# A decode step of attention and MLP on one core: first load ahead of the engines' parts, the last wait behind them, and the result turned by TensorE

## The chip, the core and the metric

The kernel runs on one NeuronCore of one Trainium2 chip. The core has five engines with instruction streams of their own: TensorE (PE; its weight loads are shown as PEld), VectorE (DVE), ScalarE (ACT), GpSimd (POOL) and SyncE (SP), which here only issues transfers. Transfers run on 16 DMA engines. The engines meet through semaphores. The metric is the device time of one execution in microseconds (us), as the median of several.

## What is computed

One token x (512 values) goes through two branches that are mixed by a gate. Branch A is attention with 32 heads over a cache of 4096 keys and values per head (head size 128); branch B is an MLP with a squared ReLU. All arrays are bfloat16.

```python
g = sigmoid((x * gate_w).sum(-1, keepdims=True))
q = (x @ wq).reshape(B, Sq, Hq, Dh)              # 512 -> 32 heads of 128
scores = einsum("bhqd,bhkd->bhqk", q, k) * (Dh ** -0.5)
p = softmax(scores, axis=-1)
a = einsum("bhqk,bhkd->bhqd", p, v).reshape(B, Sq, Hq * Dh) @ wo
h = relu(x @ w1 + b1)
b = (h * h) @ w2 + b2
return g * a + (1 - g) * b                       # 512 values, 1 KB
```

Each value of the caches is used once. What has to be read is 32 heads of 1 MB of keys and 1 MB of values, 4 MB each of `wq` and `wo`, and some 2.8 MB of MLP weights: 78.3 MB in all.

## The kernel before

Every engine's program is written out by hand, with a part for each engine inside one block (`nc.Block()`, line 248). Ahead of the block stands the opening of the program: a few constants set by GpSimd, and a meeting of all engines (line 733 in the profile). Behind the block all engines drain and meet once more; the profile shows this under line 103.

SyncE's part (lines 251 to 294) issues the large loads in the order in which they are needed: four loads of `wq` (line 254, 128 rows of 8 KB each, 1 MB), then seven heads of keys, then values and keys in turn (lines 260 and 265), with the MLP's and `wo`'s loads set in between (lines 277 to 290). Loads into a buffer in use wait for the engines that read it. At the very end SyncE waits for `s_f4`, issues the store of the result (line 292), and waits for `s_out`, which the store raises when it has landed (line 294).

ScalarE issues four small loads at the start (lines 340 to 343): x, `gate_w`, `b1`, and `b2` as 4 rows of 256 bytes. TensorE, VectorE and ScalarE work head by head: half of the scores of a head are made by VectorE (line 629), the other half by TensorE, which transposes key blocks into PSUM buffers `KP` (line 427, copied out by ScalarE at line 361) and multiplies. The sums over the values follow seven heads behind (line 463).

All terms of the result are summed in one PSUM tile `acc`, 128 x 4 (four columns of 128 values): the output projection (lines 507, 525, 531, 537) and the MLP's second layer (line 546). The last loads to land are those of `w2` (lines 287 to 290), so that line 546 comes last on TensorE.

The result is brought out by VectorE. It adds `b2` (already times 1 - g) into column 0 of each of four 32-wide groups of the tile `fin`, 128 x 4 x 32, whose rest was set to zero at line 597. Then it transposes `fin` in blocks of 32 x 32 (line 719) into `finT`, after which the wanted values stand in rows 0, 32, 64 and 96, each row with four runs of 32 values. The store gathers these 16 runs of 64 bytes.

Line 513 is a step used below for comparison: it transposes `onorm`, 128 x 8, on TensorE into 8 rows of 128 in PSUM, and VectorE copies them to SBUF at line 712.

Of the kernel before, what the change touches and what calls it, by code (L numbers as in the profile page):

```python
# [5 lines left out]
def bass_gated_mix__gqa_block_cached__dense_activation_squared_relu__decode_kernel(  # L6
# [22 lines left out]
    bf16 = mybir.dt.bfloat16  # L29
    ALU = mybir.AluOpType  # L30
# [47 lines left out]
    def turns():  # L78
        at, out = 0, []
        for _, e, k, _, _ in RUNS:  # L80
            d = (e - at) % 16
            out.append((False, d) if d != 1 else (True, e))
            at = (e + k) % 16
        return out
# [11 lines left out]
    wq_v = A_wq.rearrange("(p t) n -> p t n", t=4)  # L96
# [5 lines left out]
    ctx = ExitStack()  # L102
    with ctx:
        def sb(name, shape, dt):
            return ctx.enter_context(nc.sbuf_tensor(name, shape, dt))

        def pb(name, shape, dt):
            return ctx.enter_context(nc.psum_tensor(name, shape, dt))

        def sem(name):  # L110
            return ctx.enter_context(nc.semaphore(name))
# [4 lines left out]
        wq_sb = W[:, :].rearrange("p (t n) -> p t n", t=4)  # L116
# [17 lines left out]
        oB = sb("oB", [NH - NA, 128], bf16)  # L134
        o2A = sb("o2A", [128, 32], bf16)
        o2B = sb("o2B", [128, TB], bf16)
        finT = sb("finT", [128, 128], bf16)
        zeros = sb("zeros", [128, 128], bf16)
        xb = sb("xb", [128, 4, 128], bf16)
        dm = xb[:, :, :].rearrange("p t (n a c) -> p (t n) a c", a=2, c=16)  # L140
        ident = sb("ident", [128, 128], bf16)
# [17 lines left out]
        hr = sb("hr", [128, FG + 1], fp32)  # L159
        hs = sb("hs", [128, FG + 1], bf16)  # L160
        b2g = sb("b2g", [128, 4], fp32)
        fin = sb("fin", [128, 4, 32], bf16)

        KP = [pb(f"KP{i}", [128, HB * 128], bf16) for i in range(3)]
        pS = pb("pS", [128, 512], fp32)
# [16 lines left out]
        acc = pX[:, 256:260]  # L182
# [13 lines left out]
        s_wq = [sem(f"s_wq{t}") for t in range(4)]  # L196
# [9 lines left out]
        s_oT = sem("s_oT")  # L206
        s_oc = sem("s_oc")
        s_o2 = sem("s_o2")
        s_f4 = sem("s_f4")
        s_k = [sem(f"s_k{i}") for i in range(NK)]  # L210
        s_v = [sem(f"s_v{i}") for i in range(NV)]
# [33 lines left out]
        s_fin = sem("s_fin")  # L245
        s_out = sem("s_out")

        block = ctx.enter_context(nc.Block())


        @block.sync
        def _(eng):
            for t in range(4):
                eng.dma_start(wq_sb[:, t, :], wq_v[:, t, :]).then_inc(s_wq[t], 16)  # L254

            def load_k(h):
                if h >= NK:
                    eng.wait_ge(s_sd, h - NK + 1)
                    eng.wait_ge(s_t, 2 * (h - NK + 1))
                eng.dma_start(Kt[:, h % NK, :], k_h[h, :, :]).then_inc(s_k[h % NK], 16)  # L260

            def load_v(h):
                if h >= NV:
                    eng.wait_ge(s_pv, h - NV + 1)
                eng.dma_start(Vt[:, h % NV, :], v_h[h, :, :]).then_inc(s_v[h % NV], 16)  # L265

            for h in range(LAG):
                load_k(h)
            for h in range(NH):
                load_v(h)  # L270
                if h + LAG < NH:
                    load_k(h + LAG)
                if h == HF:
                    eng.wait_ge(s_qps, 8)
                if HF <= h < HF + len(FIRST):
                    p, st, k, q = STRIPS[len(RUNS) + h - HF]
                    eng.dma_start(W[p:p + st * (k - 1) + 1:st, :], woa_v[q:q + k, :],
                                  max_dma_last_dim=8192).then_inc(s_wr, 16)
                if h == 8:
                    eng.wait_ge(s_z, 1)  # L280
                    eng.wait_ge(s_b2, 1)
                    for t in range(4):
                        eng.dma_start(w1_sb[:, t, :], w1_v[:, t, :]).then_inc(s_w1, 16)
            eng.wait_ge(s_sd, NA + 2)
            eng.wait_ge(s_t, 2 * (NA + 2))
            eng.dma_start(wob_sb[:, :, :], wob_v.rearrange("p (t n) -> p t n", n=DM)).then_inc(s_wo, 16)
            eng.dma_start(w2a[:, 0:GS[1], :], w2_v[:, 0:GS[1], :]).then_inc(s_w2[0], 16)
            eng.dma_start(wox, A_wo[HX * 128:NA * 128, :]).then_inc(s_wx, 16)
            eng.dma_start(w2b[:, :], B_w2[FG * 128:F, :]).then_inc(s_w2[1], 16)
            eng.dma_start(w2a[:, GS[1]:FG, :], w2_v[:, GS[1]:FG, :]).then_inc(s_w2[2], 16)  # L290
            eng.wait_ge(s_f4, 1)
            eng.dma_start(out[0, 0, :].rearrange("(j k a) -> k j a", j=4, k=4),
                          finT[0:97:32, :].rearrange("k (j a) -> k j a", j=4)).then_inc(s_out, 16)
            eng.wait_ge(s_out, 16)


        @block.gpsimd
# [89 lines left out]
        def _(eng):  # L387
# [152 lines left out]
            def mlp_out(c):  # L540
                eng.wait_ge(s_w2[c], 16)
                for n in [range(GS[1]), [FG], range(GS[1], FG)][c]:
                    M = 128 if n < FG else FR
                    w = w2a[:, n, :] if n < FG else w2b[:, :]
                    for j in range(4):
                        mm = eng.matmul(acc[:, j:j + 1], w[:, j * 128:(j + 1) * 128], hs[0:M, n:n + 1],  # L546
                                        start=False, stop=(n == FG - 1), skip_group_check=True)
                if c == 2:
                    mm.then_inc(s_acc, 1)
# [39 lines left out]
            out_x()  # L589
            mlp_out(1)  # L590
            mlp_out(2)


        @block.vector
        def _(eng):
            eng.memset(zeros[:, :], 0.0).then_inc(s_dz, 1)
            eng.memset(fin[:, :, :], 0.0).then_inc(s_fin, 1)
            eng.wait_ge(s_dz, 1)
            eng.wait_ge(s_x, 32)
            eng.tensor_tensor_reduce(grow, xrow, grow, 1.0, 0.0, ALU.mult,  # L600
# [113 lines left out]
            eng.tensor_copy(o2B[:, :], O2B).then_inc(s_o2, 1)  # L714
            eng.wait_ge(s_acc, 1)
            eng.wait_ge(s_g, 4)
            eng.tensor_tensor(fin[:, :, 0], acc[:, 0:4], b2g[:, :], ALU.add).then_inc(s_fin, 1)
            eng.wait_ge(s_fin, 2)
            eng.transpose(finT[:, :], fin[:, :, :].rearrange("p j a -> p (j a)")).then_inc(s_f4, 1)


# [26 lines left out]
```

## Time and profile before

| what | us |
|---|---|
| median of 3 runs (lowest, highest) | 198.02 (198.01, 198.27) |
| the profiled execution | 198.08 |
| its span, first to last instruction | 196.3 |
| VectorE busy | 139.5 |
| TensorE busy | 132.9 |
| ScalarE busy | 79.5 |
| GpSimd busy | 29.9 |
| loads of keys and values, median from issue to landing | 27.2 |

The DMA engines moved 78.76 MB at a mean of 401 GB/s over the span. A line of a timeline gives the start and the length in us, the engine (with q for its queue of transfers and semaphores), the line of the kernel, the operation, what it writes and reads, and in brackets how long the engine stood idle before it and which instruction or transfer released it. A line of a one-line view gives the shortest, median and longest duration in ns and the first and last start. In the windows view each line is a stretch: its length, the busy time of each engine with its count of instructions, the granted TensorE clock as a share of full speed, the mean share of the 16 DMA engines that is busy, and what they moved.

### The profile page before, as it was taken

How to read it: one execution, taken by the hardware profiler on the slowest of the kernel's cores; microseconds unless marked ns; L12 is line 12 of the kernel's file. 1: busy time of each engine (PE TensorE's matmuls, PEld its weight loads, DVE VectorE, ACT ScalarE, POOL GpSimd, SP SyncE). 2: the span in 40 equal slices, each digit the busy share in tenths (PEclk: the TensorE clock that was granted, in tenths of full speed). 3: DMA queues.
4: the chain of work that ended last, by engine and by line, in shares of the span. 5: the costliest groups of instructions: out<-in, count | busy, mean ns of one | idle time of the engine just before them, and what ended most of it. 6: DMA issues, size and time to landing. Idle time of an engine off the chain costs nothing.

```text
span 196.3 us, 6564 instructions
## 1 busy us (share of the span) xinstructions
PE 132.9 (68%) x2402; PEld 118.8 (61%) x2408; DVE 139.5 (71%) x1152; ACT 79.5 (41%) x148; POOL 29.9 (15%) x53
## 2 busy tenths in 40 slices
PE   0128756699876867806697760769998677785872
PEld 0105725578675667706676760668997666785862
DVE  0307999999998687707877871777779999949310
ACT  2105838356473536503356330633077334611000
POOL 2000000000000000000019940000099750000000
PEclk9999978555585555665555555555555555555555
DMA  6999999999999999999999999999999999999990
GB/s 226 425 427 426 416 416 426 419 422 416 411 422 422 412 417 407 423 421 417 421 416 421 416 414 409 409 409 414 413 416 416 426 412 422 419 417 414 416 351 28
DMA packets 12730, 78.76 MB, mean 401 GB/s; under 512 B 2502, under 2 KB 2728, under 8 KB 3369
## 3 DMA queue, kind: packets, MB, share of 16 engines
q1 hardware_dynamic: 11146, 75.77, 93.6%
q0 software_dynamic: 1536, 2.56, 3.5%
q8 instruction: 19, 0.31, 0.6%
q14 instruction: 15, 0.11, 0.2%
q10 hardware_dynamic: 14, 0.01, 0.0%
HBM read 78.32 MB, written 0.00 MB: 399 GB/s over the span
## 4 chain that ended last, share of the span: by engine, by line
DMA 59%; DVE 22%; PE 9%; SPq 6%; issue 3%; ACT 0%
DMA Kt<-in_A_k_cache_dram 42%; DVE Kt L629 18%; DMA w2a<-in_B_w_dram 12%; DMA W<-in_A_wq_dram 6%; SPq L265 4%; PE KP L427 3%; PE pX L481 2%; DVE S L629 1%; SPq L260 1%; PE pQ L405 1%; PE pX L477 1%; PE pX L546 1%; SPq L254 1%; PE pS L438 1%; DVE dg L644 0%
## 5 line engine op out<-in xcount | busy, mean ns | idle before, releaser
L629 DVE CUSTOM_DVE_ANT_0 Kt<-Kt,qb 128x128 bf16<-128x128 bf16 x512 | 113.3, 289 | 23.2 <-DMA Kt<-in_A_k_cache_dram 23.2
L361 ACT ACTIVATE kT<-KP 128x1024 bf16<-128x1024 bf16 x64 | 61.8, 1021 | 68.8 <-PE KP L427 68.8
L427 PE MATMUL KP<-ident,Kt 128*128 128x128 bf16 x512 | 56.8, 300 | 32.8 <-DMA Kt<-in_A_k_cache_dram 32.8
L427 PEld LDWEIGHTS KP<-ident,Kt 128*128 128x128 bf16 x512 | 49.5, 140 | 35.6 <-DMA Kt<-in_A_k_cache_dram 34.4
L629 DVE DVE_READ_ACCUMULATOR2_ANT S<- 128x1 f32 x512 | 41.0, 80 | 0.0
L438 PEld LDWEIGHTS pS<-qcol,kT 128*128 128x128 bf16 x512 | 18.5, 107 | 10.7 <-DVE S L635 10.5
L438 PE MATMUL pS<-qcol,kT 128*128 128x1 bf16 x512 | 19.1, 167 | 8.4 <-DVE S L635 8.2
L315 POOL DMA_DIRECT2D xb<-in_B_w_dram x9 | 5.3, 590 | 100.3 <-PE pQ L405 100.3
L405 PE MATMUL pQ<-W,xb 128*128 128x512 bf16 x26 | 12.4, 620 | 7.8 <-DMA W<-in_A_wq_dram 6.4
L463 PEld LDWEIGHTS pO<-E,Vt 128*128 128x128 bf16 x512 | 15.5, 104 | 1.1 <-issue 0.8
L463 PE MATMUL pO<-E,Vt 128*128 128x1 bf16 x512 | 16.1, 165 | 0.0
L333 POOL TENSOR_SCALAR_AFFINE_SELECT w_sb<-w_sb 24x36 bf16<-24x36 bf16 (+5 forms) x19 | 11.0, 578 | 2.7
L353 ACT ACTIVATE qb<-pQ 128x512 bf16<-128x512 f32 x8 | 4.7, 591 | 14.9 <-PE pQ L405 14.9
L405 PEld LDWEIGHTS pQ<-W,xb 128*128 128x128 bf16 x32 | 3.6, 130 | 10.8 <-issue 10.8
L372 ACT ACTIVATE E<-S,nM 128x32 bf16<-128x32 f32 x32 | 9.9, 309 | 0.3
L463 PE MATMUL pQ<-E,Vt 128*128 128x1 bf16 x256 | 8.1, 165 | 2.3 <-DMA Vt<-in_A_v_cache_dram 2.0
L463 PEld LDWEIGHTS pQ<-E,Vt 128*128 128x128 bf16 x256 | 7.7, 104 | 2.5 <-issue 2.4
L463 PEld LDWEIGHTS pX<-E,Vt 128*128 128x128 bf16 x256 | 7.7, 103 | 0.5 <-issue 0.2
L463 PE MATMUL pX<-E,Vt 128*128 128x1 bf16 x256 | 8.0, 165 | 0.0
L318 POOL DMA_DIRECT2D W<-in_A_wo_dram x14 | 7.8, 563 | 0.0
L615 DVE CAST qcol<-pQ 128x4 bf16<-128x4 f32 x8 | 1.2, 152 | 8.4 <-PE pQ L413 8.4
L635 DVE COPY S<-pS 128x16 f32<-128x16 f32 x32 | 5.4, 168 | 2.2 <-PE pS L438 2.2
(84 smaller groups left out, 93.0 us busy)
## 6 DMA issues: line engine op xcount, KB each, us to landing
Kt<-in_A_k_cache_dram SPq DMA_DIRECT2D x32, 1024.0 KB, 27.2
Vt<-in_A_v_cache_dram SPq DMA_DIRECT2D x32, 1024.0 KB, 27.2
W<-in_A_wq_dram SPq DMA_DIRECT2D x4, 1024.0 KB, 7.9
W<-in_A_wo_dram POOLq DMA_DIRECT2D x2, 768.0 KB, 12.8
w_sb<-in_B_w_dram SPq DMA_DIRECT2D x4, 344.0 KB, 22.9
Kt<-in_A_wo_dram SPq DMA_DIRECT2D x1, 1024.0 KB, 21.5
w2a<-in_B_w_dram SPq DMA_DIRECT2D x1, 1024.0 KB, 23.3
W<-in_A_wo_dram POOLq DMA_DIRECT2D x10, 64.0 KB, 23.5
```

The lines of the kernel that those rows point to most:

```text
L265: eng.dma_start(Vt[:, h % NV, :], v_h[h, :, :]).then_inc(s_v[h % NV], 16)
L315: eng.dma_start(dm[0:d, sent, :, 0:8], src[:, :, 0:8]).then_inc(s_dm[sent], 16)
L318: eng.dma_start(W[p:p + st * (k - 1) + 1:st, :], woa_v[q:q + k, :], max_dma_last_dim=8192).then_inc(s_wp[n], 16)
L333: eng.affine_select(out=part, in_=part, compare_op=ALU.not_equal, fill=1.0, base=-st * q, pattern=[[st, 4], [-1, st * (k - 1) + 1]], chann ...
L361: eng.activation(kT[:, h % 2, j * HB * 128:(j + 1) * HB * 128], KP[n % 3][:, :], ACT.Copy).then_inc(s_ev, 1)
L372: eng.activation(E[:, h % NE, :], S[:, h % NS, :], ACT.Exp, bias=nM[:, h:h + 1], scale=SCALE, accum_out=RS[:, h:h + 1]).then_inc(s_e, 1)
L405: mm = eng.matmul(pQ[:, :], xb[:, t, :], wq_sb[:, t, c * 512:(c + 1) * 512], start=(t == 0), stop=(t == 3))
L427: mm = eng.transpose(KP[n % 3][:, y * 128:(y + 1) * 128], Kt[:, h % NK, b * 128:(b + 1) * 128], ident[:, :])
L438: mm = eng.matmul(S2[:, y:y + 1], kT[:, h % 2, y * 128:(y + 1) * 128], qcol[:, h:h + 1], start=True, stop=True)
L463: mm = eng.matmul(O(h, h + 1), Vt[:, h % NV, b * 128:(b + 1) * 128], E[:, h % NE, b:b + 1], start=(b == 0), stop=(b == NB - 1))
L629: ins = eng.tensor_tensor_reduce(kb, kb, qb[:, h * 128:(h + 1) * 128], 1.0, 0.0, ALU.mult, ALU.add, S[:, h % NS, b:b + 1])
L635: eng.tensor_copy(S[:, h % NS, XB:NB], S2).then_inc(s_cp, 1)
```

## The change

The first of the four `wq` loads is issued by SyncE ahead of the block, that is before its program enters its part; the loop in the part starts at 1. The block is opened and closed by an `ExitStack` of its own, and SyncE's wait for the store stands behind its closing, after the drains and the meeting of all engines. `fin` becomes 128 x 4 and is no longer cleared; TensorE transposes it into 4 rows of 128 in `KP[1]`, VectorE copies them to `fin4`, and the store writes 4 rows of 256 bytes.

```diff
-        finT = sb("finT", [128, 128], bf16)
+        fin4 = sb("fin4", [4, 128], bf16)
...
-        fin = sb("fin", [128, 4, 32], bf16)
+        fin = sb("fin", [128, 4], bf16)
...
+        s_fT = sem("s_fT")
...
-        block = ctx.enter_context(nc.Block())
-
+        nc.sync.dma_start(wq_sb[:, 0, :], wq_v[:, 0, :]).then_inc(s_wq[0], 16)
+
+        body = ExitStack()
+        block = body.enter_context(nc.Block())
 
         @block.sync
         def _(eng):
-            for t in range(4):
+            for t in range(1, 4):
                 eng.dma_start(wq_sb[:, t, :], wq_v[:, t, :]).then_inc(s_wq[t], 16)
...
             eng.wait_ge(s_f4, 1)
-            eng.dma_start(out[0, 0, :].rearrange("(j k a) -> k j a", j=4, k=4),
-                          finT[0:97:32, :].rearrange("k (j a) -> k j a", j=4)).then_inc(s_out, 16)
-            eng.wait_ge(s_out, 16)
+            eng.dma_start(out[0, 0, :].rearrange("(j p) -> j p", p=128), fin4[:, :]).then_inc(s_out, 16)
...
             mlp_out(2)
+            eng.wait_ge(s_fin, 1)
+            eng.transpose(KP[1][0:4, 0:128], fin[:, :], ident[:, :]).then_inc(s_fT, 1)
...
             eng.memset(zeros[:, :], 0.0).then_inc(s_dz, 1)
-            eng.memset(fin[:, :, :], 0.0).then_inc(s_fin, 1)
...
-            eng.tensor_tensor(fin[:, :, 0], acc[:, 0:4], b2g[:, :], ALU.add).then_inc(s_fin, 1)
-            eng.wait_ge(s_fin, 2)
-            eng.transpose(finT[:, :], fin[:, :, :].rearrange("p j a -> p (j a)")).then_inc(s_f4, 1)
+            eng.tensor_tensor(fin[:, :], acc[:, 0:4], b2g[:, :], ALU.add).then_inc(s_fin, 1)
+            eng.wait_ge(s_fT, 1)
+            eng.tensor_copy(fin4[:, :], KP[1][0:4, 0:128]).then_inc(s_f4, 1)
+
+        body.close()
+        nc.sync.wait_ge(s_out, 16)
```

## The prediction

> **What bounds the kernel now.** I read the windows view first, to see which resource sets each stretch, then the timeline of the end, the waits of SyncE's queue, and the one-line views of the instructions that the change touches.
>
> ```profile
> core 0: us, PE busy (x) PEld busy (x) DVE busy (x) ACT busy (x) POOL busy (x), PEclk, DMA share, GB/s
> 0.00:4.90 4.90, 0.00 (x0) 0.00 (x0) 0.19 (x2) 1.28 (x1) 1.25 (x9) 1.00 0.64 224
> 4.90:50.00 45.10, 29.07 (x392) 22.85 (x394) 35.37 (x318) 22.52 (x36) 0.00 (x0) 0.79 1.01 422
> 150.00:190.00 40.00, 30.27 (x690) 28.14 (x688) 30.91 (x204) 12.40 (x28) 8.25 (x19) 0.50 1.01 416
> 192.00:194.20 2.20, 1.44 (x48) 1.38 (x48) 0.49 (x2) 0.00 (x0) 0.00 (x0) 0.50 0.08 26
> 194.20:196.30 2.10, 0.00 (x0) 0.00 (x0) 0.00 (x0) 0.00 (x0) 0.00 (x0) 0.50 0.01 0
> ```
>
> From 5 us to 190 us the DMA share is 1.01 at 416 to 422 GB/s: the loads never pause, so this stretch can only be moved, not shortened, by what the diff touches. What is left is the start, before the first bytes, and the end, in which DMA and all engines are all but idle (the last two rows).
>
> ```profile
> 192.14 0.99 PE L546 MATMUL pX<-hs,w2a 128*128 128x1 bf16 x32 [0.82 <-DMA w2a<-in_B_w_dram]
> 193.20 0.37 PE L546 MATMUL pX<-hs,w2a 128*128 128x1 bf16 x8
> 193.61 0.17 DVE L717 TENSOR_TENSOR fin<-pX,b2g 128x4 bf16<-128x4 f32 x1 [3.90 <-PE pX L546]
> 193.82 0.31 DVE L719 STREAM_TRANSPOSE finT<-fin 128x128 bf16<-128x128 bf16 x1
> 194.16 0.65 SPq L292 DMA_DIRECT2D out_dram<-finT  x1
> ```
>
> TensorE waits for the last loads until 192.14 and works to 193.57. VectorE then adds (to 193.78) and transposes (to 194.13), and SyncE issues the store from 194.16 to 194.81. All in a row: each of these is on the path.
>
> ```profile
> SPq L103 <- DMA out_dram<-finT: 1.1, 1, 1.1
> SPq L103 <- PEq L103: 0.2, 1, 0.2
> ...
> L103 POOLq EVENT_SEMAPHORE  x2: 17/17/17, 196.1 to 196.2; - x2
> L103 PEldq DRAIN  x1: 405/405/405, 193.2 to 193.2; - x1
> L103 SPq COMPARE_BRANCH  x1: 32/32/32, 195.9 to 195.9; - x1
> L103 SPq DRAIN  x1: 7/7/7, 196.1 to 196.1; - x1
> L103 SPq EVENT_SEMAPHORE  x1: 17/17/17, 196.2 to 196.2; - x1
> ```
>
> After its issue SyncE waits 1.1 us, until 195.9, for the store to land. Only then come its branch (195.9), its drain (196.1) and the meeting of all engines (the semaphore instructions to 196.2); the span ends at 196.3. So 0.4 us of ending follow the landing. The profiled execution took 198.08 us, 1.8 us more than its span; the median is 0.06 below it.
>
> **The wait moved behind the end.** SyncE now goes from the store's issue straight to the drain and the meeting, and waits for the landing after them. The 0.4 us then run under the store's flight (1.1 us, less what the store gains below), which covers them more than once. The wait keeps a check of its own, 0.05 us at most by the 0.017 to 0.032 us of the rows above. I take −0.35; the bounds are −0.40 and 0, the latter if the drain itself held until the landing. Behind the waiting instruction nothing is queued but the end of the program.
>
> **The turn.** The same work stands in the trace for a matrix of 8 columns:
>
> ```profile
> 188.06 0.23 DVE L656 SCALAR_TENSOR_TENSOR onorm<-pQ,gcol,rden 128x8 bf16<-128x8 f32 x1 [3.16 <-PE pQ L463]
> 188.34 0.27 PE L513 MATMUL KP<-ident,onorm 128*8 128x128 bf16 x1 [0.39 <-DVE onorm L656]
> 188.65 0.21 DVE L712 COPY oB<-KP 8x128 bf16<-8x128 bf16 x1 [0.36 <-PE KP L513]
> 189.54 0.17 DVE L714 CAST o2B<-pS 128x8 bf16<-128x8 f32 x1 [0.68 <-PE pS L516]
> ```
>
> From the end of VectorE's result (188.29) over TensorE's transpose to the end of the copy (188.86) it is 0.57 us, at the same granted clock, 0.50, as at the end. It replaces the way from 193.78 to 194.13, 0.35 us. So +0.22; with a copy between 0.17 and 0.25 us, +0.18 to +0.26. TensorE's new wait for the sum has nothing behind it but its drain; VectorE's wait for TensorE has the copy behind it, and SyncE's store waits for that, which is the path just counted. The PSUM buffer was last read for the last keys, long before. The clearing of the result tile falls away:
>
> ```profile
> 0.90 0.11 DVE L597 MEMSET fin<- 128x64 uint32 x1
> ...
> 5.60 0.68 DVE L600 CUSTOM_DVE_ANT_0 w_sb<-w_sb 1x512 bf16<-1x512 bf16 x1 [4.59 <-DMA w_sb<-in_gate_w_dram]
> ```
>
> VectorE then idles 4.59 us for a load of ScalarE's, so it is worth nothing, and 0.1 us if that idle time were gone.
>
> **The store.** It is the same 1 KB, in 4 rows of 256 bytes instead of 16 pieces in two dimensions. How long does such a shape take?
>
> ```profile
> L254 SPq DMA_DIRECT2D W<-in_A_wq_dram x4: 383/427/625, 0.7 to 2.1; - x4
> L265 SPq DMA_DIRECT2D Vt<-in_A_v_cache_dram x32: 327/2124/7253, 6.7 to 167.3; - x32
> L277 SPq DMA_DIRECT2D W<-in_A_wo_dram x5: 739/936/2459, 119.2 to 143.1; - x5
> L340 ACTq DMA_DIRECT2D w_sb<-in_A_x_dram x1: 526/526/526, 0.7 to 0.7; - x1
> L343 ACTq DMA_DIRECT2D w_sb<-in_B_b_dram x1: 264/264/264, 1.8 to 1.8; - x1
> ```
>
> L343 loads 4 rows of 256 bytes, the new shape, and its issue took 0.26 us. L265 issues 128 plain rows in 0.33 at its shortest, after a wait. L277 cuts its rows into pieces, 8 to 12 of them, and never took under 0.74. So it is the pieces within a row that cost, not the count, and the store's 0.65 belongs to that family: −0.39 by the issue alone. ScalarE's first issue (L340, one row, 0.53) hints at a cost of a long-idle queue instead, which would leave the store as it is. What counts is when the bytes move:
>
> ```profile
> GB/s 0 0 0 0 0 0 0 0 0 0 0 0 0 0 0 0 0 0 0 20 0 328 492 164 328 328 328 0 0 164 328 164 0 164 0 0 328 164 328 328
> ...
> GB/s 0 0 0 0 0 0 0 0 0 0 0 0 0 0 0 0 0 0 0 0 0 0 0 0 0 14 5 0 0 0 0 0 0 0 0 0 0 0 0 0
> DMA packets 20, 0.00 MB, mean 0 GB/s; under 512 B 20, under 2 KB 20, under 8 KB 20
> ```
>
> The first row cuts 0.7 to 2.7 us into 40 slices of 0.05: the row issued at 0.74 moves at 1.65 (20 GB/s), the 128 rows issued at 0.74 from 1.75; 0.91 and 1.01 us from the start of the issue. The second cuts 194.0 to 196.3 into slices of 0.0575: the store's bytes move from 195.44, 1.28 us from its issue. With a start as for plain rows the store gains 0.27 to 0.37 us. I take −0.33, between these and the issue's −0.39. The bytes spread over two slices, 0.1 us; four packets instead of 16 save 0 to 0.05, I take −0.03. From below both may be nothing.
>
> Of the 1.7 us from issue to landing, the last bytes' own way takes about 0.4 (195.5 to 195.9). The Trainium skill (DMA: Bandwidth & Descriptors, "Latency and other measured facts") says the other way round that the receipt of the write is most of a small transfer's fixed cost. By that rule the shape is worth little and the whole sum would be −0.15; the trace, with 1.28 of 1.7 ahead of the bytes, does not agree.
>
> **The first load.** It is one issue of 128 rows, 1 MB. It is moved past SyncE's own way into its part and, on the chip's DMA engines, past nothing that was ahead of it.
>
> ```profile
> 0.68 0.06 issue
> 0.74 0.38 SPq L254
> 1.13 0.06 issue
> 1.19 0.42 SPq L254
> ```
>
> SyncE leaves the opening meeting at 0.68 and issues at 0.74; the gap to its second issue is 0.06 too. So there is 0.06 to win at the very most, 0 at the least; I take −0.02. Whatever it wins shifts the whole stretch of full DMA share, and so the end. Loads 2 to 4 may come later without harm, since the first has data for some 2.4 us (1 MB at 422 GB/s).
>
> The Trainium skill (Advanced Engine Details and Errata, "Control Flow Timing") gives a plain branch about 51 ns. By that rule this term would be −0.05, and the sum −0.54; no row here shows such a branch at the entry.
>
> **The sum**, against the profiled execution: +0.22 − 0.33 − 0.03 − 0.35 − 0.02 = −0.51, so 197.57 us there and, 0.06 lower, **197.5** as a median. Bounds of all terms together: +0.26 to −0.72.
>
> **Rivals.** (1) The store stays as slow, because its 0.65 us is that of a store or of a queue idle for 20 us. L340 speaks for it; the 0.33 of L265 after its waits, and L277, against. The terms −0.36 go: −0.15, 197.9.
>
> (2) The moved wait gains nothing, because SyncE's drain holds until the store has landed. TensorE's drain, begun at 193.2 with the last matmuls still running, took 0.405, so a drain can wait for work under way; SyncE's 0.007 was seen only with nothing under way. The term −0.35 goes: −0.16, 197.9.
>
> (3) More is won than the span shows. Of the 1.8 us around the span some follow the meeting. The other engines would leave it at about 194.9 (the store issued from 194.16 + 0.22, for 0.26; then the meeting, 0.2 to 0.3) while SyncE's wait ends at about 195.8: 0.9 us ahead. If what follows is set by them, I estimate half of that: −0.5 more, 197.0. The trace has no row behind the meeting, so nothing speaks against it but that SyncE may itself be last.
>
> (4) Slower: TensorE's two new instructions are not on hand. TensorE's program is fetched in pieces during the run; one such fetch stands right here:
>
> ```profile
> DMA packets 1, 0.02 MB, mean 14 GB/s; under 512 B 0, under 2 KB 0, under 8 KB 0
> ...
> q8 instruction: 1, 0.02, 5.5%
> ```
>
> This is the window 193.0 to 194.2: 5.5% of 16 engines over 1.2 us is one packet of 1.06 us, begun at 193.08 or so. If the transpose had to wait for a fetch of its own, the end would come 1.06 later: −0.51 + 1.06 = +0.55, 198.6 us; it decides the sign from a stall of 0.51. Against it: the drain that follows the last matmul in TensorE's program was issued at 193.2, while that fetch ran, so the instructions behind the matmuls were there. The Trainium skill (Runtime: NRT & Kernel Launch, "Instruction fetch mechanics") names another place for such a stall, a taken branch out of the loaded pages; at the entry it would be covered by the first load's 2.4 us.
>
> **How the numbers follow.** A change of 0.2%, 0.40 us, is about what a measurement of this kernel can tell from none. The forecast has 0.54 (its own range 197.3 to 197.7, with 0.47 below 197.62 and 0.07 above), rival 1 has 0.10, rival 2 has 0.05, rival 3 has 0.17, rival 4 has 0.14. Faster: 0.47 + 0.17 = 0.64; the same: 0.07 + 0.15 = 0.22; slower: 0.14. The range 196.95 to 198.1 leaves out rival 4 and the lower third of rival 3.
>
> **What would show it.** Right: the store's issue at about 0.26 us, its bytes 0.9 to 1.0 us from the issue's start; the drains and semaphores of the end standing ahead of the store's landing; the way from the sum to the issue at about 0.6 us; the first load at 0.72 and the DMA share unchanged. The forecast is wrong if the store's issue stays at 0.65, if SyncE's drain lasts until the landing, if the time falls by clearly more than the span, or if TensorE's transpose starts later than 0.1 us after the sum.

## The result, and the profile after

The changed kernel takes 197.03 us (196.79 to 197.08, 4 runs) against 198.15 us (198.01 to 198.32) of the kernel before in the same comparison: a ratio of 0.9943, with a 95% interval of 0.9931 to 0.9955. That is 1.12 us less, where the forecast's sum was 0.51. The profiled execution took 196.79 us with a span of 195.4, so that 1.4 us lie around the span now, where it was 1.8.

First the windows view of the changed kernel, to be laid beside the one of before:

```profile
0.00:4.90 4.90, 0.00 (x0) 0.00 (x0) 0.11 (x1) 1.28 (x1) 1.25 (x9) 1.00 0.65 226
4.90:50.00 45.10, 27.77 (x394) 21.60 (x394) 35.44 (x318) 22.49 (x36) 0.00 (x0) 0.80 1.01 421
150.00:190.00 40.00, 30.03 (x689) 27.91 (x687) 30.90 (x204) 12.17 (x28) 8.23 (x19) 0.50 1.01 416
192.00:194.20 2.20, 1.69 (x49) 1.43 (x49) 0.37 (x2) 0.00 (x0) 0.00 (x0) 0.50 0.08 25
194.20:195.40 1.20, 0.00 (x0) 0.00 (x0) 0.00 (x0) 0.00 (x0) 0.00 (x0) 0.50 0.01 1
```

Up to 190 us nothing has changed: the same DMA share of 1.01 at the same rate. The difference is in the last row, the time in which no engine computes: 1.2 us instead of 2.1. The timeline of this end:

```profile
193.07 0.36 PE L547 MATMUL pX<-hs,w2a 128*128 128x1 bf16 x8
193.47 0.16 DVE L719 TENSOR_TENSOR fin<-pX,b2g 128x4 bf16<-128x4 f32 x1 [3.77 <-PE pX L547]
193.68 0.08 PEld L594 LDWEIGHTS KP<-ident,fin 128*4 128x4 bf16 x1 [0.34 <-DVE fin L719]
193.69 0.26 PE L594 MATMUL KP<-ident,fin 128*4 128x128 bf16 x1 [0.25 <-DVE fin L719]
193.99 0.21 DVE L721 COPY fin<-KP 4x128 bf16<-4x128 bf16 x1 [0.36 <-PE KP L594]
194.23 0.29 SPq L295 DMA_DIRECT2D out_dram<-fin  x1
```

VectorE's sum starts at 193.47, 0.14 us earlier than in the profile of before, because the last loads landed that much earlier in this execution; the spans of the changed kernel's four runs are 195.4 to 195.7, so this is scatter. From the start of the sum to the store's issue it is 0.76 us instead of 0.55. The issue itself takes 0.29 us instead of 0.65. Then the end, as the waits of SyncE's queue and the one-line views of lines 723 and 724 show it:

```profile
SPq L724 <- DMA out_dram<-fin: 0.4, 1, 0.4
SPq L723 <- PEq L723: 0.2, 1, 0.2
...
L723 POOLq EVENT_SEMAPHORE  x2: 17/17/17, 194.8 to 194.9; - x2
L723 SPq DRAIN  x1: 206/206/206, 194.6 to 194.6; - x1
L723 PEldq EVENT_SEMAPHORE  x1: 51/51/51, 194.9 to 194.9; - x1
L724 SPq EVENT_SEMAPHORE  x1: 17/17/17, 195.4 to 195.4; - x1
```

SyncE drains right after the issue, for 0.2 us; the engines meet at 194.9; only SyncE stays to 195.4 for the landing. The view of transfers, 194.0 to 196.3 us in slices of 0.0575, has the store's bytes in the 18th slice, from 194.98, 0.75 us from the start of the issue instead of 1.28:

```profile
GB/s 0 0 0 0 0 0 0 0 0 0 0 0 0 0 0 0 0 14 5 0 0 0 0 0 0 0 0 0 0 0 0 0 0 0 0 0 0 0 0 0
DMA packets 8, 0.00 MB, mean 0 GB/s; under 512 B 8, under 2 KB 8, under 8 KB 8
```

And the start, from the chain of waits:

```profile
0.68 0.06 issue
0.74 0.39 SPq L249
1.13 0.06 issue
1.19 0.41 SPq L257
```

The first load, now line 249, is issued at 0.74 and the second at 1.19, as before. Moving it won nothing.

In the span this gives: turn +0.21, store from issue to landing 1.71 to 1.17 (−0.54), landing to the end of the span 0.41 to 0.03 (−0.38), together −0.71. Some 0.4 us more went from outside the span, where no row stands: to a hundredth, 1.80 us lay there before and 1.36 lie there now. Which part of the change took them was the first question.

### The profile page after: what moved, and what is told of

It is laid out like the page before. It is cut to its first block, busy times and chain, and to the rows that moved or that the text cites. A ratio compares the mean times of both kernels' runs of the same rounds, so it can differ in the third digit from the quotient of the medians.

```text
span 195.4 us, 6571 instructions
## 1 busy us (share of the span) xinstructions
PE 132.8 (68%) x2409; PEld 117.3 (60%) x2409; DVE 139.5 (71%) x1151; ACT 79.4 (41%) x148; POOL 29.9 (15%) x53
## 4 chain that ended last, share of the span: by engine, by line
DMA 59%; DVE 22%; PE 9%; SPq 6%; issue 3%; ACT 0%
DMA Kt<-in_A_k_cache_dram 42%; DVE Kt L631 19%; DMA w2a<-in_B_w_dram 12%; DMA W<-in_A_wq_dram 6%; SPq L268 4%; PE KP L428 3%; PE pX L482 2%; DVE S L631 1%; SPq L263 1%; PE pQ L406 1%; PE pX L478 1%; PE pX L547 1%; PE pS L439 1%; DVE dg L646 1%; DVE S L637 0%
## 5 line engine op out<-in xcount | busy, mean ns | idle before, releaser
L428 PE MATMUL KP<-ident,Kt 128*128 128x128 bf16 x512 | 55.2, 294 | 32.0 <-DMA Kt<-in_A_k_cache_dram 32.0
L428 PEld LDWEIGHTS KP<-ident,Kt 128*128 128x128 bf16 x512 | 47.9, 137 | 34.4 <-DMA Kt<-in_A_k_cache_dram 33.6
L406 PE MATMUL pQ<-W,xb 128*128 128x512 bf16 x32 | 14.5, 609 | 6.4 <-DMA W<-in_A_wq_dram 6.4
```

The costliest lines, as they stand in the source:

```text
L406: mm = eng.matmul(pQ[:, :], xb[:, t, :], wq_sb[:, t, c * 512:(c + 1) * 512], start=(t == 0), stop=(t == 3))
L428: mm = eng.transpose(KP[n % 3][:, y * 128:(y + 1) * 128], Kt[:, h % NK, b * 128:(b + 1) * 128], ident[:, :])
```

## The experiments

Two theories went in. A: these 0.4 us come from the moved wait, since the other engines are past the meeting before SyncE is. B: they come from the first load, issued before SyncE enters its part. The first four runs stand against the kernel before at 198.19 us.

### e1: only the wait moved

```diff
-        block = ctx.enter_context(nc.Block())
+        body = ExitStack()
+        block = body.enter_context(nc.Block())
...
-            eng.wait_ge(s_out, 16)
...
+        body.close()
+        nc.sync.wait_ge(s_out, 16)
```

> The kernel before, with only SyncE's wait for the store moved behind the end. In the span the 0.38 us between the store's landing and the end should go, by every theory. The changed kernel also has 1.38 us around its span where the kernel before has 1.78. Theory A: these 0.40 us come from the moved wait (the other engines are past the meeting early, and what follows on them was last): then 197.4 us, with about 1.4 around the span. Theory B: they come from the first load issued ahead: then 197.8 us, with 1.8 around the span. In both, the store keeps an issue of 0.65 us and 1.7 us to its landing.

Measured: 197.38 us, ratio 0.9963 (0.9950 to 0.9976); span 195.9 in a profiled execution of 197.36, so 1.4 us around it. Theory A. Its end, with the old store:

```profile
194.18 0.65 SPq L293 DMA_DIRECT2D out_dram<-finT  x1
...
L721 SPq DRAIN  x1: 467/467/467, 194.9 to 194.9; - x1
L721 PEldq EVENT_SEMAPHORE  x1: 51/51/51, 195.5 to 195.5; - x1
L722 SPq EVENT_SEMAPHORE  x1: 17/17/17, 195.9 to 195.9; - x1
```

Behind the old store SyncE's drain takes 0.47 us, behind the new one 0.21. It is over before the first bytes move: at 195.35 here, with the bytes from 195.47, and at 194.78 in the changed kernel, with the bytes from 194.98. In both it ends 0.10 us after the trace records the first raise of the store's semaphore. So the drain waits for part of the store's work, though not for its landing.

### e2: only the first load moved

```diff
+        nc.sync.dma_start(wq_sb[:, 0, :], wq_v[:, 0, :]).then_inc(s_wq[0], 16)
+
         block = ctx.enter_context(nc.Block())
...
-            for t in range(4):
+            for t in range(1, 4):
```

> The kernel before, with only the first load issued ahead of the block. Theory A: nothing changes, 198.1 us, first issue at 0.74 us, 1.8 us around the span. Theory B: 1.4 us around the span and 197.75 us, with the span as before.

Measured: 198.07 us, ratio 0.9995 (0.9985 to 1.0004), span 196.3 of 198.06. Theory B falls; the load is worth nothing that can be told.

### e3: only the turn and the 4 rows

The changed kernel's lines for `fin`, the transpose, the copy and the store, with the first load and the wait left as before.

> The kernel before, with only the turn on TensorE and the store of 4 rows. Theory A and B alike: the way to the issue +0.21 us, issue to landing 1.17 instead of 1.71 us (-0.54), so -0.33 in the span, 1.8 around it: 197.8 us. If the short flight of the store came from what follows it in the changed kernel (no wait of SyncE in its way) and not from its shape, it stays at 1.7 us and the time is 198.35.

Measured: 197.68 us, ratio 0.9979 (0.9970 to 0.9989), which holds the expected −0.33 us; span 195.8 of 197.59. SyncE waits for the landing inside the block here, and the way from issue to landing is as short:

```profile
L292 SPq DMA_DIRECT2D out_dram<-fin x1: 292/292/292, 194.2 to 194.2; - x1
...
L103 SPq COMPARE_BRANCH  x1: 38/38/38, 195.4 to 195.4; - x1
L103 PEldq EVENT_SEMAPHORE  x1: 51/51/51, 195.7 to 195.7; - x1
```

From the issue at 194.2 to the branch at 195.4 it is 1.18 us in the trace's records. The shorter flight belongs to the store, not to what follows it.

### e4: the meeting made late, which missed

```diff
             eng.tensor_copy(fin4[:, :], KP[1][0:4, 0:128]).then_inc(s_f4, 1)
+            for i in range(16):
+                eng.memset(junk[:, 8 * i:8 * i + 8], 0.0)
```

> The changed kernel, with 16 small clearings of an unused tile on VectorE behind its last copy (some 1 us), so that the meeting of all engines ends about when the store lands and the other engines have no lead over SyncE's wait. The span stays (195.4 to 195.7 us), the store is untouched. Theory A, with the lead as its cause: the 0.40 us come back, 1.8 us around the span, 197.4 us. Rival: what is won around the span is SyncE's own (it ends with a wait instead of a meeting), whatever the lead: 1.4 around the span, 197.0 us.

Measured: 197.00 us, ratio 0.9941 (0.9924 to 0.9957). The edit did not do what it was to do. The 16 clearings of 62 ns each were issued mostly about 11 ns apart and done at 194.8, before SyncE's drain:

```profile
194.48 0.28 DVE L724 MEMSET junk<- 128x4 uint32 x16
194.56 0.29 SPq L296 DMA_DIRECT2D out_dram<-fin  x1
...
L726 SPq DRAIN  x1: 206/206/206, 194.9 to 194.9; - x1
```

From the store's issue to the meeting's end it is 0.77 us, as in the changed kernel, so the meeting moved by nothing. This run tells the theories apart in no way. But laying the six profiles so far side by side showed a rule: the time was always 1.80 us more than the end of the meeting, counted from the span's start, whether SyncE was still waiting for the store (the changed kernel, e1, e4) or not. That made two new theories. L: the meeting sets the end, and the store's landing has left the path. M: SyncE's last wait sets it.

### e5: the meeting made late by larger clearings

```diff
             eng.tensor_copy(fin4[:, :], KP[1][0:4, 0:128]).then_inc(s_f4, 1)
+            for i in range(2):
+                eng.memset(qb[:, 1024 * i:1024 * i + 1024], 0.0)
```

> The changed kernel with two clearings of 128 x 1024 values of the spent tile qb on VectorE behind its last copy, some 0.53 us each, so that VectorE's drain and the meeting come about 0.5 us later (the clearings of e4 ran ahead of SyncE's drain and moved nothing). In all six profiles so far the execution ended 1.80 us after the end of the meeting, however late SyncE's wait for the store ended. Theory L, the meeting rules: the store's landing stays at about 1.17 us from its issue and does not matter; the end is 1.80 us after the later meeting, 0.5 later than the changed kernel: 197.5 us, 1.8 around the span if the meeting ends last. Theory M, SyncE's last wait rules (1.36 to 1.43 us before the end): the span's end moves by 0.1 us at most, so 197.0 to 197.1 us.

Measured: 197.43 us, ratio 0.9972 (0.9961 to 0.9983) against 198.01 us of the kernel before beside it. The profiled execution of 197.58 us:

```profile
194.48 0.29 SPq L295 DMA_DIRECT2D out_dram<-fin  x1
194.51 1.02 DVE L723 MEMSET qb<- 128x512 uint32 x2
...
L725 DVEq DRAIN  x1: 1311/1311/1311, 194.3 to 194.3; - x1
L725 SPq DRAIN  x1: 246/246/246, 194.8 to 194.8; - x1
L725 PEldq EVENT_SEMAPHORE  x1: 51/51/51, 195.7 to 195.7; - x1
L726 SPq EVENT_SEMAPHORE  x1: 17/17/17, 195.8 to 195.8; - x1
```

VectorE's drain holds the meeting to 195.7, and SyncE's wait passes right behind it, the store having landed at 195.64. The end follows the meeting, 1.79 us later, and not SyncE's wait, behind which it comes 1.75 us later here and 1.36 to 1.43 in the changed kernel, e1 and e4. That is theory L's number.

### e6: 16 pieces from the same 4 rows

```diff
-        fin4 = sb("fin4", [4, 128], bf16)
+        fin4 = sb("fin4", [4, 4, 40], bf16)
...
-            eng.dma_start(out[0, 0, :].rearrange("(j p) -> j p", p=128), fin4[:, :]).then_inc(s_out, 16)
+            eng.dma_start(out[0, 0, :].rearrange("(j k a) -> j k a", j=4, k=4),
+                          fin4[:, :, 0:32]).then_inc(s_out, 16)
```

(The copy writes the four runs in the same way.)

> The changed kernel with its 4 rows kept in four runs of 64 bytes with gaps between, so that the store has 16 pieces again, from 4 neighbouring rows. If the pieces are what the old store's shape cost: issue 0.65 us, a long drain of SyncE as in e1 (0.47 instead of 0.21 us), the meeting 0.6 us later: 197.6 us, as e1 with the turn's 0.21 added. If the rows 0, 32, 64 and 96 as the source or VectorE's transpose were the cost: issue 0.29 us and 197.0 us.

Measured: 197.57 us, ratio 0.9980 (0.9970 to 0.9989).

```profile
L295 SPq DMA_DIRECT2D out_dram<-fin x1: 751/751/751, 194.2 to 194.2; - x1
...
L724 SPq DRAIN  x1: 478/478/478, 195.0 to 195.0; - x1
```

With TensorE's turn kept and only the runs cut, the long issue and the long drain are back. The shape was the cost, not the spread rows or VectorE's transpose.

### e7 and e8: the store, then the whole tail behind the meeting

In e7 the wait for `s_f4` and the store stand behind `body.close()`; in e8 TensorE's `mlp_out`, `out_x` and the turn, and VectorE's sum and copy, stand there too.

```diff
         body.close()
+        nc.sync.wait_ge(s_f4, 1)
+        nc.sync.dma_start(out[0, 0, :].rearrange("(j p) -> j p", p=128), fin4[:, :]).then_inc(s_out, 16)
         nc.sync.wait_ge(s_out, 16)
```

> The changed kernel with the store itself issued behind the meeting, not only the wait for it. The meeting then waits for VectorE's drain (194.25 us) instead of SyncE's (194.78): 0.53 us earlier. Theory L: 196.5 us, if SyncE's own ending fits into what is left behind its wait. Theory M: SyncE leaves the meeting at about 194.45, issues 0.2 us later than now, and everything follows: 197.25 us.

> As e7, and TensorE's last layer, its turn and VectorE's last steps stand behind the meeting too, so that the meeting (at about 191 us) is off the path. The store is issued as in the changed kernel. Theory L can't hold to the letter (191 + 1.8 is before the store): what binds next is each engine's own end; with 1.8 us behind VectorE's copy (194.2) 196.2 us in the median. Theory M: SyncE's wait ends where it does now, 197.0 us.

Measured: e7 197.11 us, ratio 0.9954 (0.9940 to 0.9969); e8 196.85 us, ratio 0.9942 (0.9927 to 0.9957). Neither is theory L's 196.5 or 196.2. e7's store:

```profile
194.63 0.29 SPq L723 DMA_DIRECT2D out_dram<-fin  x1
...
L724 SPq EVENT_SEMAPHORE  x1: 17/17/17, 195.8 to 195.8; - x1
```

and e8's:

```profile
194.43 0.29 SPq L727 DMA_DIRECT2D out_dram<-fin  x1
...
L712 PEldq EVENT_SEMAPHORE  x1: 51/51/51, 191.3 to 191.3; - x1
L728 SPq EVENT_SEMAPHORE  x1: 17/17/17, 195.6 to 195.6; - x1
```

In e7 the meeting is at 194.6, in e8 at 191.3, well off the path; the profiled executions (197.13 and 196.94 us) end 1.30 us after SyncE's last instruction. So both theories are half right. A table of all profiled executions, in us, with the ends of the meeting and of SyncE's last instruction taken from the same records to a hundredth:

| kernel | time | meeting ends | SyncE ends | time less meeting | time less SyncE |
|---|---|---|---|---|---|
| before | 198.08 | 196.28 | 196.23 | 1.80 | 1.85 |
| changed | 196.79 | 194.99 | 195.43 | 1.80 | 1.36 |
| e1 | 197.36 | 195.56 | 195.93 | 1.80 | 1.43 |
| e2 | 198.06 | 196.25 | 196.21 | 1.81 | 1.85 |
| e3 | 197.59 | 195.79 | 195.75 | 1.80 | 1.84 |
| e4 | 197.13 | 195.33 | 195.76 | 1.80 | 1.37 |
| e5 | 197.58 | 195.79 | 195.83 | 1.79 | 1.75 |
| e6 | 197.48 | 195.67 | 196.04 | 1.81 | 1.44 |
| e7 | 197.13 | 194.62 | 195.83 | 2.51 | 1.30 |
| e8 | 196.94 | 191.35 | 195.63 | 5.59 | 1.31 |
| e9 | 196.85 | 195.04 | 195.47 | 1.81 | 1.38 |
| e10 | 196.93 | 191.26 | 195.62 | 5.67 | 1.31 |
| e11 | 197.71 | 195.91 | 196.26 | 1.80 | 1.45 |

The last two columns also hold whatever lies ahead of the span's first instruction; no record splits it off. By the table the execution ends at the later of two: 1.80 us after the meeting, or 1.30 us after SyncE's last instruction. The 1.30 rests on e7, e8 and e10 alone. In these three the store's issue, its landing 1.17 us later and SyncE's wait 0.03 us behind that stand at fixed distances, so that which of them starts the 1.30 is not shown. In the changed kernel they are 196.79 and 196.73: SyncE's wait is 0.06 us short of costing something. What the program does in these 1.80 and 1.30 us no record shows.

### e9, e10, e11: the changed kernel beside e8, and 8 pieces

e9 is the changed kernel and e10 the kernel of e8, on one chip; e11 is e6 with `fin4` as 4 x 2 x 80 and two runs of 64 values in each row.

> The changed kernel itself, beside the next run. All ten profiles so far fit one rule: the execution ends at the later of 1.80 us after the meeting and 1.30 us after SyncE's last instruction. Here both come within 0.1 us of each other: 1.1 us below the kernel before.

> The kernel of e8 on the same chip as e9. By the rule of the two ends only the 0.06 us by which the meeting rules in the changed kernel are to be had: the same within 0.1 us. If the meeting alone ruled, as theory L had it, this would be some 0.5 us or more below e9.

> As e6, with two runs of 128 bytes in each of the 4 rows: 8 pieces. If each piece beyond the first of a row costs the same, issue and drain lie a third of the way from the changed kernel's (0.29 + 0.21 us) to e6's (0.75 + 0.48): some 0.74 us together, the meeting 0.24 later: 197.25 us. If any second dimension costs the full price: 197.6 us.

Measured, against 198.11 us: e9 196.85 us, ratio 0.9937 (0.9923 to 0.9950); e10 196.83 us, ratio 0.9939 (0.9927 to 0.9952); e11 197.60 us, ratio 0.9974 (0.9964 to 0.9984). e10 beats e9 by nothing that can be told, as the rule of two ends says: nothing found here is faster than the changed kernel. And in e11:

```profile
L295 SPq DMA_DIRECT2D out_dram<-fin x1: 744/744/744, 194.4 to 194.4; - x1
...
L724 SPq DRAIN  x1: 472/472/472, 195.2 to 195.2; - x1
```

8 pieces cost what 16 do. It is the second dimension that is dear, not the number of pieces. Nor is it that the pieces are small, as far as a load may stand for a store: the loads of line 277, which the trace records as 4 x 2 or 4 x 3 pieces of 8 KB, never took under 0.74 us to issue either.

## Why the prediction was right in sign and too small

**What bounds the kernel:** right. The stretch of full DMA share kept its length and its rate; all that was won lies behind the last loads.

**The turn, +0.22:** right, +0.21. TensorE began 0.05 us after the sum ended (193.63 to 193.68). Rival 4, a missing instruction, did not come.

**The store, −0.33 and −0.03:** right in kind, too small. Together they measured −0.54, nearly all of it ahead of the first byte; the bytes themselves take some 0.09 us in both kernels. I took the issue's shortening (−0.36 measured, −0.39 predicted) as the bound of the gain. But the bytes also started sooner behind the end of the issue, 0.47 instead of 0.64 us. The start of plain loads, 0.91 and 1.01 us from the issue, was too careful a yardstick for a row store: 0.75. Rival 1 fell with e3 and e6. By the receipt rule of the Trainium skill (DMA: Bandwidth & Descriptors, "Latency and other measured facts") the sum would have been −0.15. The trace does not agree: the way from the last bytes to the landing is some 0.34 us in both kernels, and the shape moved what lies ahead of the first byte, 1.28 to 0.75 us.

**The wait, −0.35:** the step that failed. Inside the span it is right (−0.38). The mistake was to let the span's end stand for the end of the execution: what lies behind it was taken as fixed for the forecast and left to rival 3. In the trace of before the meeting is last, and the 1.80 us outside the span are counted from it. Once the wait stands behind the meeting, it is the meeting that counts, and it no longer waits for the landing. e1, this part alone, measured −0.81 us where the term had −0.35. Rival 3 named this, with 197.0 us and a chance of 0.17. Its working was off in two places that cancelled: the lead of the other engines is 0.44 us, not 0.9, since the meeting waits for SyncE's drain, which the working put at nothing, and since the store lands sooner; and all of it counts (1.80 less 1.36), not half. That rival 3's time fits, and with it that the range reached down far enough, is luck as far as the number goes. Rival 2 was half right: the drain does last longer behind the store, 0.21 us instead of 0.007, but it does not hold until the landing.

**The first load, −0.02:** nothing (e2), as the lower bound had it. The issue stands at 0.74 us in both, behind the opening meeting. The Trainium skill (Advanced Engine Details and Errata, "Control Flow Timing") gives a plain branch about 51 ns. They are not seen here: the gap ahead of the first issue is 0.06 us with the load on either side of SyncE's way into its part.

Put together by the path that decides, the meeting: from the store's issue to the meeting's end it was 2.12 us before (194.16 to 196.28) and is 0.77 now (194.23 to 194.99), −1.35; with the turn's +0.21 that is −1.14, against −1.12 measured. On the same path e1 has −0.74 and e3 −0.32, together −1.06. The times of the single parts add to more (−0.81 in e1, −0.12 in e2, −0.51 in e3), but their intervals allow for that: e3's alone reaches from −0.22 to −0.59. In the changed kernel the landing does not occur on this path any more, and the store's shape counts through issue and drain (0.65 + 0.47 in e1, 0.29 + 0.21 here) instead of through its flight.

## What to carry to other kernels

A wait for the last store can stand behind the closing meeting of the engines; here it ended 0.44 us after the meeting at no cost, and by the two figures found the limit is 0.5 (1.80 less 1.30). Look at time less span in each profile, and ask which engine's last instruction starts that rest. A small store should be a plain list of rows: here it was worth an extra 0.2 us of computing to get there (e3). A load written ahead of the engines' parts, but behind the opening meeting, starts no earlier; one ahead of that meeting was not tried.

## What the runs showed of the hardware that was not expected

SyncE's drain behind an issued store is not free: 0.21 us behind 4 rows (0.25 in e5), 0.47 to 0.48 behind 8 or 16 pieces, 0.007 once the store has landed. A store of 8 pieces in two dimensions takes as long to issue (0.74 us) as one of 16 (0.75), and both take 2.5 times the 0.29 of 4 rows. Sixteen small clearings on VectorE, 62 ns each, were issued mostly 11 ns apart (e4), so that they filled 0.3 us and not 1.
